# A gated-MLP kernel with attention ahead of it: the residual stream is remade from its normalized rows, which are turned by VectorE

## The chip, the cores and the metric

The kernel runs on one core of a Trainium2 chip. The metric is the device time of one execution in microseconds; several executions are timed and their median is told. A core has TensorE (PE, with a view of its own, PEld, for its weight loads), VectorE (DVE), ScalarE (ACT), GpSimd (POOL) and SyncE (SP), which here only issues DMA transfers. On-chip memory is SBUF (128 partitions) and PSUM, into which PE writes.

## The reference

Attention over a sliding window of 256 positions, its output projection, a residual, a layer norm, and a gated MLP whose gate mixes positions with a 2048 x 2048 matrix. The sizes are S = 2048 positions, D = 640, H = 32 heads, F = 1728 and Fh = F / 2 = 864; everything is float32.

```python
o = softmax(mask(q @ k.T * Dh ** -0.5)) @ v          # 32 heads, window 256
h = x + o @ wo                                       # residual stream
hn = _layernorm(h)
z = _gelu(hn @ w_in)
z1, z2 = z[..., :Fh], _layernorm(z[..., Fh:])
g = einsum("ts,bsf->btf", w_sp, z2) + b_sp
out = h + (z1 * g) @ w_out
```

h is used twice: normalized as the input of the MLP, and raw at the very end.

## The kernel before

Positions are worked in NT = 16 tiles of P = 128 rows; D is KD = 5 blocks of 128 columns. Each large product is made of three matmuls on parts: a number is split into a high part (a copy rounded to the matmul's format, by ACT) and a low part (the difference, mostly by VectorE), and high x high, high x low and low x high are summed. Some products are also cut into 2 x 2 blocks and done in seven products instead of eight, which needs sums and differences of blocks ahead of the split.

The stages, with their times in the profiled execution: attention up to 458.3 us, in a fixed order; then

- the projection (458.3 to 546.7), the loop over tiles i at lines 1325 to 1359. Tile i takes 30 matmuls (L96) into `wo_ps`, a PSUM accumulator of which there are three (`acc_tile`). VectorE adds x to it and makes the row sum in one instruction (L1345), which gives h in `xh` (five buffers, each reloaded with x, L142). ACT squares for the variance (L1348) and POOL takes the root (L1351). ACT writes the normalized rows hn(i) (L1356) into a buffer that is free by then: `rows[0]` or `rows[1]`, a quarter of `fx`, at the end `rows[2]`, `rows[3]`. h goes to DRAM as `h_d` on ACT's queue (L1349). The next tiles' o is loaded (L150), normalized (L166) and split (ACT L174, VectorE L175, into `xb`) in the same loop;
- three tiles later, `turn_h(i)` (L847) transposes hn(i) by five PE transposes (L856) into a PSUM tile of its own (`aux`, one buffer), ACT copies that to `ho` (L857, shown as L723), and SP stores it as `hn_d` (L858). The last three tiles are turned among the first z products;
- the z pairs 0 to 7 (`z_pair`, L872; 546.7 to 635.4) load two tiles of `hn_d` into quarters of `fx` (L889, L890), build sums, high and low parts in `aw`, multiply with `win1` (`zl`, made from w_in in the projection stage by `win1_prep`), apply the gelu and store z1;
- the z2 pairs 8 to 12 (`z2_pair`, L949; 635.4 to 692.1) do the same for the other half of w_in, load at L977, and make a layer norm of the result;
- the first gate (`first_gate`, to 825.8), the z2 pairs 13 to 15 (to 877), the second gate with the output projection (`second_gate`, `final`; to 1108.2), in which `load_h` (L1225) brings h back for the last sum. `turn_y` transposes the gated rows for the output projection and splits them (L137).

The order is written as steps. `at(n, f)` puts work f at step n; each step then issues its product. From the projection on, the framework orders the instructions of each engine by its own estimates of their durations, and every engine runs its list in that order. SP's list has all loads and nearly all stores; a DMA that stands behind one which still waits for its data waits as well. SP's DMAs go over eight completion lanes in turn. The 13th pair is special: its loads stand five steps ahead of its first product (`soon`), and its preparation one step ahead, since its buffers are not free earlier.

## Time and profile before

| | us |
|---|---|
| median of three executions | 1111.19 (1108.33 to 1111.58) |
| the profiled execution: its span from the first to the last instruction | 1108.2 |
| what lies around the span, by the median | 2.99 |
| projection stage | 88.4 |
| z pairs 0 to 7 | 88.7 |
| z2 pairs 8 to 12 | 56.7 |
| first gate | 133.7 |
| z2 pairs 13 to 15 | 51.2 |
| second gate and output | 231.2 |

The profile gives a span and no other time of its execution. The page shows, among other things, the busy share of each engine in 40 equal slices (27.7 us each; a digit is tenths, 9 is 90% or more); PEclk is the granted clock of TensorE:

```profile
PE   9999999999999999989999999999999999999998
DVE  6541212879999998677567478676637985566543
ACT  4333433249999999567776567433326531122210
POOL 3114444457777778512100055256422000000000
PEclk9999999999999999999999999999999999999999
DMA  7212565565666654678755421447593663444321
```

Slices 17 to 20 are the projection, 21 to 24 the z pairs. And the costliest transfers of hn_d and h_d, as the page's list of DMA issues has them (what, how many, KB each):

```profile
fx<-hn_d SPq DMA_DIRECT2D x32, 320.0 KB
```

### The profile page before, as it was taken

The page shows a single profiled execution, that of the slowest core. Times are in us where ns is not written, and L with a number is a line of the kernel's source. Part 1 is how long each engine was busy: PE and PEld are TensorE (multiplying, and loading weights), DVE is VectorE, ACT ScalarE, POOL GpSimd, SP SyncE. Part 2 cuts the span into 40 slices and gives each one's busy share as a digit, 9 for nine tenths or more (in the row PEclk, how much of TensorE's full clock was granted, in tenths as well). Part 3 has the DMA queues.
Part 4 walks back from the last instruction along what each step waited for, and adds up shares of the span by engine and source line. Part 5 has one row for each costly group of instructions (what it writes and reads, how often), then busy time and mean ns, then how long its engine had stood idle before and what let it go on. Part 6 is the DMA issues. An engine that isn't in the chain of part 4 may idle for free.

```text
span 1108.2 us, 27795 instructions
## 1 busy us (share of the span) xinstructions
PE 1084.3 (98%) x10667; PEld 974.4 (88%) x10667; DVE 720.7 (65%) x2043; ACT 571.0 (52%) x1215; POOL 369.6 (33%) x524
## 2 busy tenths in 40 slices
PE   9999999999999999989999999999999999999998
PEld 7998877668888877788899999999999999999998
DVE  6541212879999998677567478676637985566543
ACT  4333433249999999567776567433326531122210
POOL 3114444457777778512100055256422000000000
PEclk9999999999999999999999999999999999999999
DMA  7212565565666654678755421447593663444321
GB/s 261 74 35 96 166 221 179 196 210 181 214 204 214 215 177 120 193 254 281 242 188 193 151 80 39 165 154 233 190 339 113 204 215 114 129 132 150 100 91 65
DMA packets 88501, 187.80 MB, mean 169 GB/s; under 512 B 11648, under 2 KB 48144, under 8 KB 84448
## 3 DMA queue, kind: packets, MB, share of 16 engines
q1 hardware_dynamic: 83728, 172.08, 47.8%
q0 software_dynamic: 2336, 8.70, 2.2%
q10 hardware_dynamic: 2304, 5.24, 1.2%
q8 instruction: 84, 1.38, 0.5%
q14 instruction: 49, 0.40, 0.1%
HBM read 121.66 MB, written 65.52 MB: 169 GB/s over the span
## 4 chain that ended last, share of the span: by engine, by line
PE 78%; DMA 8%; DVE 3%; issue 3%; POOL 3%; ACT 3%; SPq 2%; ACTq 0%; POOLq 0%; DVEq 0%
PE g L1165 20%; PE zb L968 9%; PE out_ps L1218 8%; PE pv L435 6%; PE bank L341 5%; PE bank L407 5%; PE zx L916 3%; PE zv L916 2%; PE qk L525 2%; PE qk L526 2%; PE qk L527 2%; DMA qk_d<-sg 2%; PE zy L916 2%; SPq L320 1%; PE zw L916 1%
## 5 line engine op out<-in xcount | busy, mean ns | idle before, releaser
L410 ACT ACTIVATE pt<-bank 128x384 f32<-128x384 f32 (+2 forms) x512 | 200.8, 496 | 10.4 <-PE bank L407 5.7
L1165 PE MATMUL g<-zl,aw 128*128 128x432 f32 x768 | 169.7, 359 | 0.0
L353 DVE CUSTOM_DVE_ANT_0 junk<-bank,strip 128x288 bf16<-128x288 f32 x392 | 157.7, 454 | 4.3 <-PE bank L341 3.0
L723 ACT ACTIVATE aw<-fx 128x512 fp32r<-128x512 f32 (+2 forms) x147 | 84.9, 592 | 141.1 <-PE g L1165 101.9
L1165 PEld LDWEIGHTS g<-zl,aw 128*128 128x128 f32 x768 | 143.5, 188 | 6.1
L1165 PE MATMUL g<-ze,aw 128*128 128x432 f32 x576 | 131.9, 359 | 1.1 <-DVE row L717 1.1
L435 PE MATMUL pv<-pt,v_sb 128*32 128x192 f32 (+3 forms) x1984 | 127.3, 323 | 3.8 <-POOL pt L415 1.3
L717 DVE TENSOR_TENSOR aw<-fx,aw 128x512 fp32r<-128x512 f32 (+2 forms) x146 | 99.4, 690 | 28.6 <-ACT aw L723 23.5
L1165 PEld LDWEIGHTS g<-ze,aw 128*128 128x128 f32 x576 | 107.1, 188 | 6.2 <-DVE row L717 1.8
L407 PE MATMUL bank<-slot 123*32 123x288 bf16 (+5 forms) x1536 | 106.1, 282 | 1.0 <-ACT pt L410 0.4
L412 POOL TENSOR_SCALAR_AFFINE_SELECT pt<-pt 128x512 f32<-128x512 f32 x128 | 82.9, 648 | 43.6 <-ACT pt L410 42.4
L1218 PE MATMUL out_ps<-wout,y_sp 128*128 128x320 f32 (+1 forms) x630 | 96.4, 309 | 0.4 <-ACT y_sp L137 0.4
L968 PE MATMUL zb<-win,aw 128*128 128x432 f32 x480 | 95.0, 359 | 0.5 <-ACT aw L723 0.5
L1218 PEld LDWEIGHTS out_ps<-wout,y_sp 128*128 128x128 f32 (+1 forms) x630 | 94.2, 188 | 1.0 <-ACT y_sp L137 0.7
L968 PEld LDWEIGHTS zb<-win,aw 128*128 128x128 f32 x480 | 90.1, 188 | 5.0 <-ACT aw L723 0.9
L341 PE MATMUL bank<-slot 120*32 120x288 bf16 (+2 forms) x1264 | 89.8, 285 | 1.1 <-DVE mcol L353 1.0
L541 DVE TENSOR_TENSOR rest<-qk,sg 128x512 f32<-128x512 f32 x40 | 27.7, 692 | 86.1 <-ACT sg L539 86.1
L415 POOL TENSOR_SCALAR_AFFINE_SELECT pt<-pt 128x512 f32<-128x512 f32 x112 | 74.6, 666 | 0.0
L717 DVE TENSOR_TENSOR row<-g,row 128x432 f32<-128x432 f32 x80 | 48.2, 603 | 33.8 <-PE g L1165 30.3
L544 POOL TENSOR_TENSOR sg<-rest,sg 128x512 bf16<-128x512 f32 x40 | 46.6, 1166 | 69.2 <-ACT sg L543 60.2
L435 PEld LDWEIGHTS pv<-pt,v_sb 128*32 128x32 f32 x1984 | 59.5, 110 | 10.3 <-POOL pt L415 3.2
L407 PEld LDWEIGHTS <-slot 123*32 123x32 bf16 x1536 | 52.6, 96 | 16.2 <-issue 5.0
(216 smaller groups left out, 2195.1 us busy)
## 6 DMA issues: line engine op xcount, KB each, us to landing
fx<-wsp_in SPq DMA_DIRECT2D x30, 512.0 KB
slot<-qk_d SPq DMA_DIRECT2D x72, 200.0 KB
qk_d<-sg SPq DMA_DIRECT2D x32, 384.0 KB
slot<-qk_d SPq DMA_DIRECT2D x72, 160.0 KB
fx<-hn_d SPq DMA_DIRECT2D x32, 320.0 KB
o_d<-ot SPq DMA_DIRECT2D x64, 128.0 KB
z_d<-row SPq DMA_DIRECT2D x18, 432.0 KB
g_d<-row SPq DMA_DIRECT2D x16, 432.0 KB
```

What stands on the lines that cost most here:

```text
L341: nc.tensor.matmul(ps[32 * j:32 * j + 32, :n], part(st, half, 120, 0, hh, q0, 32), part(st, half, 120, 1, hh, lo + skip * j, n), start=Tru ...
L353: nc.vector.tensor_tensor_reduce(out=junk[:, :n], in0=ps[:, :n], in1=keep, scale=1.0, scalar=NEG, op0=OP.add, op1=OP.max, accum_out=m_cols ...
L407: nc.tensor.matmul(ps[32 * i:32 * i + 32, b:e], part(st, half, 123, 1, hh, k0, 32), part(st, half, 123, 0, hh, kb * P + b, e - b), start=T ...
L410: nc.scalar.activation(pt[:, hh, :n], ps[:, :n], AF.Exp, scale=SCALE)
L412: nc.gpsimd.affine_select(out=pt[:, :, :P], in_=pt[:, :, :P], pattern=[[0, 4], [1, P]], base=0, channel_multiplier=-1, compare_op=OP.is_ge ...
L435: nc.tensor.matmul(ps[32 * hh:32 * hh + 32, a - 512 * c:b - 512 * c], v_sb[:, kb, v0:v0 + 32], pt[:, hh, a - kb * P:b - kb * P], start=fir ...
L717: (eng or nc.vector).tensor_tensor(out=out, in0=a, in1=b, op=op)
L723: nc.scalar.activation(out, a, AF.Copy)
L916: nc.tensor.matmul(ps, a[x], b[:, y], start=start and m + x + y == 0, stop=stop and m == n - 1 and x == 1, skip_group_check=True)
L968: nc.tensor.matmul(b[0][:, :HF], a[t][:, x, kk], win2[0][:, y, kk, h * HF:(h + 1) * HF], start=kk + x + y == 0, stop=kk == KD - 1 and x == 1)
L1165: nc.tensor.matmul(ps, w[m][x][:, k], zc[k][m][:, y], start=start and k + x + y == 0, stop=stop and k == 3 and x == 1, skip_group_check=True)
L1218: nc.tensor.matmul(ps[j][:, :HD], src[:w, a, k, :], e1["wout"][:w, b, k, j * HD:(j + 1) * HD], start=(k == 0 and a + b == 0), stop=(k == K ...
```

## The change

h is no longer stored. Its mean and the reciprocal of its scale factor are kept per row in `hstat`, and at the end h is remade from the stored normalized rows as hn x std + mean, on ACT (`make_h`), in the buffer into which `load_h` now loads hn. The transposition by PE, its PSUM tile and `ho` go; the accumulators become four. The normalized rows are stored by one DMA right after they are made (`store_hn`) into an `hn_d` of four column bands of 160, so that each contiguous run is 640 bytes. A load (`load_hn`) is now four DMAs of 32 partitions each, one for each band; they place the four 32-row groups so that VectorE's transposition in blocks of 32 x 32 over the whole 128 x 640 buffer (`turn`) leaves the wanted columns on the partitions, in another order of columns. Readers take that order through a view of four dimensions (`turned`, `cols`), and the rows of w_in are reordered on the host to match. In `z_pair` the load moves from step 4q - 5 to 4q - 7 at the earliest and the turns get steps of their own; in `z2_pair` the turn precedes the high part. In `second_gate` `make_h` stands one to three steps behind its load.

```diff
     r_d = dram.tile([H, S], F32, name="r_d")
-    h_d = dram.tile([NT, P, D], F32, name="h_d")
     z1_d = dram.tile([NT, P, FH], F32, name="z1_d")
-    hn_d = dram.tile([NT, P, D], F32, name="hn_d")
+    hn_d = dram.tile([NT, 4, P, D // 4], F32, name="hn_d")
     g_d = dram.tile([NT, P, FH], F32, name="g_d")
...
     ones = const.tile([P, 2], F32, name="ones")
+    hstat = const.tile([P, 2, NT], F32, name="hstat")
...
     def acc_tile(name):
-        return pools["c"].tile([P, 2, 512], F32, tag="acc", bufs=3, name=name)
-
-    def aux_tile(name):
-        return pools["c"].tile([P, 2, 512], F32, tag="aux", bufs=1, name=name)
+        return pools["c"].tile([P, 2, 512], F32, tag="acc", bufs=4, name=name)
...
     mem["xh"].append(ep.tile([P, D], F32, name="xh4"))
-    mem["ho"] = [ep.tile([P, D], F32, name=f"ho{i}") for i in range(3)]
...
-    def turn_h(i):
-        ht = mem["ho"][i % 3]
-        if i < NT - 3:
-            ps = aux_tile(f"ht_ps{i}").rearrange("p a b -> p (a b)")
-            parts = [(0, KD, ps)]
-        else:
-            parts = [(0, 4, bank("b", f"ht_a{i}")), (4, KD, bank("b", f"ht_b{i}"))]
-        for k0, k1, ps in parts:
-            for k in range(k0, k1):
-                nc.tensor.transpose(ps[:, (k - k0) * P:(k - k0 + 1) * P], hn(i)[:, k * P:(k + 1) * P], ident)
-            copy(ht[:, k0 * P:k1 * P], ps[:, :(k1 - k0) * P])
-        nc.sync.dma_start(hn_d[i], ht)
+    def hn_rows(i):
+        return hn_d[i].rearrange("b p c -> p b c")
+
+    def store_hn(i):
+        nc.sync.dma_start(hn_rows(i), hn(i).rearrange("p (b c) -> p b c", b=4))
+
+    def load_hn(r, i):
+        for b in range(4):
+            nc.sync.dma_start(r[32 * b:32 * b + 32].rearrange("j (a c) -> j a c", a=4),
+                              hn_d[i, b].rearrange("(a j) c -> j a c", a=4))
+
+    def turn(r):
+        nc.vector.transpose(r, r)
+
+    def turned(r, k0=0, k1=KD):
+        return r.rearrange("p (a k j) -> p k a j", a=4, k=KD)[:, k0:k1]
+
+    def cols(t):
+        return t.rearrange("p (k a j) -> p k a j", a=4, j=32)
...
         s1 = view(fx, 4 * D, 256)
+        s1 = cols(s1)
         part = {n: (ah[:, o:o + l], al[:, o:o + l]) for n, o, l in
...
         def load():
-            nc.sync.dma_start(ri, hn_d[i])
-            nc.sync.dma_start(rj, hn_d[j])
-
-        a11, a12, a21, a22 = (r[:, o:o + 256] for r in (ri, rj) for o in (0, 256))
+            load_hn(ri, i)
+            load_hn(rj, j)
+
+        a11, a12, a21, a22 = (turned(r, k, k + 2) for r in (ri, rj) for k in (0, 2))
+
+        def hi(h, raw):
+            copy(cols(h), raw)
         def lo(h, l, raw):
-            minus(l, raw, h.bitcast(F32))
-
-        at(max(n0 - 13, 4 * q - 5), load)
-        at(max(n0 - 7, -4), lambda: copy(ah[:, :640], ri))
-        at(max(n0 - 6, -3), lambda: lo(ah[:, :640], al[:, :640], ri))
-        at(max(n0 - 5, -3), lambda: (plus(s1, a21, a22), copy(part[T1][0], s1), minus(a21, a11, a21)))
-        at(max(n0 - 4, -3), lambda: (minus(a11, s1, a11), minus(a12, a12, a11), copy(ah[:, 640:1152], ri[:, :512])))
+            minus(cols(l), raw, cols(h).bitcast(F32))
+
+        at(max(n0 - 13, 4 * q - 7), load)
+        at(max(n0 - 8, -5), lambda: turn(ri))
+        at(max(n0 - 7, -4), lambda: (turn(rj), hi(ah[:, :640], turned(ri))))
+        at(max(n0 - 6, -3), lambda: lo(ah[:, :640], al[:, :640], turned(ri)))
+        at(max(n0 - 5, -3), lambda: (plus(s1, a21, a22), hi(part[T1][0], s1), minus(a21, a11, a21)))
+        at(max(n0 - 4, -3), lambda: (minus(a11, s1, a11), minus(a12, a12, a11),
+                                     hi(ah[:, 640:1152], turned(ri, 0, 4))))
         at(n0 - 3, lambda: lo(*part[T1], s1))
-        at(n0 - 2, lambda: lo(ah[:, 640:1152], al[:, 640:1152], ri[:, :512]))
-        at(n0 - 1, lambda: copy(part[T3][0], a21))
-        at(n0, lambda: (lo(*part[T3], a21), copy(part["j"][0], rj[:, 512:])))
-        at(n0 + 1, lambda: (lo(*part["j"], rj[:, 512:]), copy(part[T4][0], a22)))
+        at(n0 - 2, lambda: lo(ah[:, 640:1152], al[:, 640:1152], turned(ri, 0, 4)))
+        at(n0 - 1, lambda: hi(part[T3][0], a21))
+        at(n0, lambda: (lo(*part[T3], a21), hi(part["j"][0], turned(rj, 4))))
+        at(n0 + 1, lambda: (lo(*part["j"], turned(rj, 4)), hi(part[T4][0], a22)))
         at(n0 + 2, lambda: lo(*part[T4], a22))
...
         def prep(t, first, eng):
-            r3 = r[t].rearrange("p (k t) -> p k t", k=KD)
+            h, l = (a[t][:, x].rearrange("p k (a j) -> p k a j", a=4) for x in range(2))
             if first:
-                copy(a[t][:, 0], r3)
+                turn(r[t])
+                copy(h, turned(r[t]))
             else:
-                minus(a[t][:, 1], r3, a[t][:, 0].bitcast(F32), eng)
+                minus(l, turned(r[t]), h.bitcast(F32), eng)
...
             soon = q == 13
-            at(m - (5 if soon else 12 if q == 8 else 6), lambda t=t, tile_t=tile_t: nc.sync.dma_start(r[t], hn_d[tile_t]))
+            at(m - (5 if soon else 12 if q == 8 else 6), lambda t=t, tile_t=tile_t: load_hn(r[t], tile_t))
             at(m - (1 if soon else 3), lambda t=t: prep(t, True, None))
...
     def load_h(n):
-        nc.sync.dma_start(e1["h"][n % 2], h_d[tile_of(n)])
+        nc.sync.dma_start(e1["h"][n % 2].rearrange("p (b c) -> p b c", b=4), hn_rows(tile_of(n)))
+
+    def make_h(n):
+        h, t = e1["h"][n % 2], tile_of(n)
+        nc.scalar.activation(h, h, AF.Identity, scale=hstat[:, 0, t:t + 1], bias=hstat[:, 1, t:t + 1])
...
         at(n0 + (11 if p == 0 else 7), lambda: load_h(j))
+        at(n0 + (11 if p == 0 else 8), lambda: make_h(i))
+        at(n0 + (13 if p == 0 else 8 if p == 7 else 10), lambda: make_h(j))
         gate_pair(p, 1, [add(11), add(22), add(12), add(12), add(22), add(11), add(21)], extra)
...
         ps = pre_ps[i] if i < 2 else proj_o(i, acc_tile(f"wo_ps{i}"))
-        if i > 2:
-            turn_h(i - 3)
         xt = hs.pop(i)
...
         nc.scalar.activation(hn(i), xt, AF.Square, bias=mv[:, 1:2], accum_out=mv[:, 2:3])
-        nc.scalar.dma_start(h_d[i], xt)
+        nc.scalar.activation(hstat[:, 1, i:i + 1], mv[:, 0:1], AF.Copy, scale=1.0 / D)
         nc.vector.tensor_scalar(out=mv[:, 2:3], in0=mv[:, 2:3], scalar1=1.0 / D, scalar2=EPS, op0=OP.mult, op1=OP.add)
...
         nc.vector.tensor_tensor(out=mv[:, 4:5], in0=mv[:, 1:2], in1=mv[:, 3:4], op=OP.mult)
+        nc.vector.reciprocal(out=hstat[:, 0, i:i + 1], in_=mv[:, 3:4])
         nc.scalar.activation(hn(i), xt, AF.Identity, scale=mv[:, 3:4], bias=mv[:, 4:5])
+        store_hn(i)
         next(w1, None)
...
         run(n)
-        if n < 3:
-            turn_h(NT - 3 + n)
         if n == 2:
...
     c = np.ascontiguousarray
+    w_in = np.asarray(B_w_in).reshape(4, KD, 32, 2 * FH).transpose(1, 0, 2, 3).reshape(D, 2 * FH)
     x = np.asarray(A_x)[0]
...
     w_out = np.pad(np.asarray(B_w_out), ((0, KF * P - FH), (0, 0)))
-    arrays = {"x_in": c(x), "wqk_in": c(wqk), "wv_in": c(wv), "wo_in": c(wo), "w_in_in": c(np.asarray(B_w_in)),
+    arrays = {"x_in": c(x), "wqk_in": c(wqk), "wv_in": c(wv), "wo_in": c(wo), "w_in_in": c(w_in),
               "wsp_in": c(wsp), "bsp_in": c(bsp), "w_out_in": c(w_out)}
...
     args = [nc.dram_tensor(n, a.shape, mybir.dt.from_np(a.dtype), kind="ExternalInput").ap()
```

Two places in the orders show what moves. The first is the end of the projection. On SP's list, where the last tiles come out, `xh` is the reload of x, `hn_d` the store of a tile's turned or, after the change, plain rows, `fx` a quarter buffer for a z pair; a row's first number is the line. Before:

```order
L142 DMA xh4_9594<-x_in 128x640
L858 DMA hn_d_70<-ho0_9595 128x640
L142 DMA xh0_8950<-x_in 128x640
L890 DMA fx_9623<-hn_d_70 128x640
L858 DMA hn_d_70<-ho1_9596 128x640
L858 DMA hn_d_70<-ho2_9597 128x640
```

After:

```order
L847 DMA hn_d_69<-fx_9620 128x4x160
L142 DMA xh2_8952<-x_in 128x640
L851 DMA fx_9620<-hn_d_69 32x4x160 x7
L847 DMA hn_d_69<-row0_9614 128x4x160
L142 DMA xh3_8953<-x_in 128x640
L851 DMA fx_9620<-hn_d_69 32x4x160
L847 DMA hn_d_69<-row1_9615 128x4x160
L142 DMA xh4_9594<-x_in 128x640
```

The stores come from the normalized rows themselves and stand between the pieces of the z pairs' loads, which now run through this part of the list in groups of four for one tile.

Still at the first place, VectorE's list at tile 13 (`mvc` are a row's statistics, `L1345` and, after the change, `L1359` the row sum of a tile). Before:

```order
L1345 ISA xh3_8953,mvc13_10343<-wo_ps13_10304,xh3_8953 128x640
L1345 ISA mvc13_10343 128x1
L717 TENSOR_TENSOR aw_9622<-fx_9623,aw_9622 128x512
L1347 TENSOR_SCALAR mvc13_10343<-mvc13_10343 128x1
L1350 TENSOR_SCALAR mvc13_10343<-mvc13_10343 128x1
L1355 TENSOR_TENSOR mvc13_10343<-mvc13_10343 128x1
L1345 ISA xh4_9594,mvc14_10394<-wo_ps14_10355,xh4_9594 128x640
```

After:

```order
L714 TENSOR_TENSOR aw_9619<-fx_9620,aw_9619 128x512
L855 STREAM_TRANSPOSE fx_9620<-fx_9620 128x640
L1364 TENSOR_SCALAR mvc12_10229<-mvc12_10229 128x1
L1359 ISA xh3_8953,mvc13_10294<-wo_ps13_10263,xh3_8953 128x640
L1359 ISA mvc13_10294 128x1
L1369 TENSOR_TENSOR mvc12_10229<-mvc12_10229 128x1
L1370 RECIPROCAL hstat_82<-mvc12_10229 128x1
L714 TENSOR_TENSOR aw_9619<-fx_9620,aw_9619 128x640
L1361 TENSOR_SCALAR mvc13_10294<-mvc13_10294 128x1
L855 STREAM_TRANSPOSE fx_9620<-fx_9620 128x640
```

A turn now stands ahead of the row sum of tile 13, and the next one ahead of that of tile 14; in all six turns stand ahead of the last row sum, at tiles 10, 11, 13, 14 and, two, 15.

The second place is pair 13, behind the first gate. It shows first on SP's list (`g_d` is the gate's store, `ze` a reload of parts that are made early). Before:

```order
L1184 DMA g_d_71<-row2_9619 128x864
L1070 DMA ze4_10532<-zp_d_75 128x864
L977 DMA fx_9623<-hn_d_70 128x640
L1185 DMA g_d_71<-row3_9620 128x864
L977 DMA fx_9623<-hn_d_70 128x640 x2
L1070 DMA ze3_10531<-zp_d_75 128x864
```

After:

```order
L1194 DMA g_d_70<-row2_9616 128x864
L1080 DMA ze4_10443<-zp_d_74 128x864
L851 DMA fx_9620<-hn_d_69 32x4x160
L1195 DMA g_d_70<-row3_9617 128x864
L851 DMA fx_9620<-hn_d_69 32x4x160 x4
L1080 DMA ze3_10442<-zp_d_74 128x864
L851 DMA fx_9620<-hn_d_69 32x4x160 x7
```

Twelve pieces stand where three loads stood, and the last seven of them stand behind the second `ze` reload, three of them pieces of the pair's second row block. It shows also on VectorE's list, where `g0_6` and `g0_7` are the gate's products in PSUM that are added into `row` and `aw` takes low parts. After:

```order
L714 TENSOR_TENSOR fx_9620<-fx_9620 128x512
L714 TENSOR_TENSOR aw_9619<-fx_9620,aw_9619 128x512 x2
L714 TENSOR_TENSOR row1_9615<-g0_7_0_0_12662,row1_9615 128x432
L714 TENSOR_TENSOR row0_9614<-g0_7_1_1_12680,row0_9614 128x432
L855 STREAM_TRANSPOSE fx_9620<-fx_9620 128x640 x2
L714 TENSOR_TENSOR aw_9619<-fx_9620,aw_9619 128x640
```

Both turns come ahead of the low part of the first block (the `aw` row behind them).

## The prediction

> **What bounds the kernel now.** I read the page's first part, then a table of busy time by stage, then what TensorE (PE) waits for in the stage that the change empties. The page first (engine, busy us, share of the span, instructions):
>
> ```profile
> span 1108.2 us, 27795 instructions
> PE 1084.3 (98%) x10667; PEld 974.4 (88%) x10667; DVE 720.7 (65%) x2043; ACT 571.0 (52%) x1215; POOL 369.6 (33%) x524
> ```
>
> PE is the bound. A change gains by taking instructions off PE or by ending PE's waits, and loses by giving PE a new wait. Where it idles is seen in the table of stages (the columns are named in its first line). The rows are: the projection, the z pairs 0 to 7, the z2 pairs 8 to 12, the first gate, the z2 pairs 13 to 15, the second gate with the output.
>
> ```profile
> core 0: us, PE busy (x) PEld busy (x) DVE busy (x) ACT busy (x) POOL busy (x), PEclk, DMA share, GB/s
> 458.30:546.70 88.40, 80.45 (x564) 77.34 (x561) 58.29 (x147) 53.58 (x95) 13.86 (x16) 1.00 0.80 262
> 546.70:635.40 88.70, 88.70 (x463) 84.90 (x461) 55.30 (x116) 57.08 (x107) 2.25 (x2) 1.00 0.54 180
> 635.40:692.10 56.70, 56.70 (x290) 54.33 (x289) 45.04 (x83) 38.80 (x69) 31.62 (x27) 1.00 0.20 64
> 692.10:825.80 133.70, 132.06 (x672) 125.55 (x671) 82.16 (x122) 49.31 (x88) 58.25 (x72) 1.00 0.61 208
> 825.80:877.00 51.20, 51.19 (x260) 48.86 (x261) 38.15 (x81) 29.54 (x49) 8.97 (x9) 1.00 0.50 176
> 877.00:1108.20 231.20, 227.33 (x1377) 221.57 (x1376) 129.28 (x245) 49.85 (x99) 0.00 (x0) 1.00 0.41 128
> ```
>
> Only the projection has idle time that this change touches: 88.40 - 80.45 = 7.95 us. The granted clock is 1.00 in every stage. The view of PE's waits in that window (what waited, for what, us in total, times, longest) puts nearly all of it down to the transposes that the change deletes:
>
> ```profile
> PE ht_ps L856 <- ACT ho L723: 4.9, 3, 2.6
> PE ht_ps L856 <- ACT row L1356: 2.8, 2, 1.9
> ```
>
> **Projection stage: what goes.** The timeline of PE (start, us, group, wait before it) gives the price of one tile's five transposes on PE:
>
> ```profile
> 490.48 0.77 PE L856 MATMUL ht_ps<-ident,row 128*128 128x128 f32 x5 [1.92 <-ACT row L1356]
> 491.00 0.82 PE L96 MATMUL wo_ps<-xb 128*128 128x320 f32 x4
> ...
> 546.23 0.77 PE L856 MATMUL ht_ps<-ident,row 128*128 128x128 f32 x5 [2.58 <-ACT ho L723]
> 546.75 1.43 PE L916 MATMUL zv<-zl,aw 128*128 128x432 f32 x6
> 548.02 0.60 PE L856 MATMUL ht_a<-ident,row 128*128 128x128 f32 x4
> ```
>
> Matmuls overlap, so the price is from start to start: 491.00 - 490.48 = 0.52 us (0.52 again at 546.23). Thirteen tiles lie in this stage: 13 x 0.52 = 6.8 us of PE work that goes. The two waits are 4.9 + 2.8 = 7.7 us. Together 14.5 us, which would leave a stage of 73.9 us. The last three tiles' transposes lie among the z products (the row at 548.02): 3 x 0.52 = **1.6 us**, on a PE that never idles there, so these go in full.
>
> **What is late next.** VectorE (DVE) gains work: a turn for each row block, and 16 reciprocals. The trace has no turn. The nearest rows of a 128x640 pass are these (group, count, busy us, mean ns, idle before):
>
> ```profile
> L86 DVE TENSOR_SCALAR xn<-xt,mva 128x640 f32<-128x640 f32 x16 | 9.8, 611 | 9.4 <-POOL mva L83 9.4
> L717 DVE TENSOR_TENSOR aw<-fx,aw 128x640 fp32r<-128x640 f32 x16 | 13.9, 871 | 14.6 <-ACT aw L723 14.6
> L1345 DVE CUSTOM_DVE_ANT_0 xh<-wo_ps,xh 128x640 f32<-128x640 f32 x16 | 13.1, 818 | 2.1 <-PE wo_ps L96 2.1
> L717 POOL TENSOR_TENSOR aw<-fx,aw 128x640 fp32r<-128x640 f32 x8 | 13.5, 1693 | 88.5 <-ACT aw L723 88.4
> L1355 DVE TENSOR_TENSOR mvc<-mvc 128x1 f32<-128x1 f32 x15 | 2.4, 157 | 4.4 <-POOL mvc L1351 4.3
> L1356 ACT ACTIVATE row<-xh,mvc 128x640 f32<-128x640 f32 x10 | 9.2, 915 | 2.3 <-DVE mvc L1355 2.0 <-DVE mvc L1350 0.2
> ```
>
> A turn is bounded by 0.61 us (VectorE's quickest pass of this shape) and 1.69 us (the slowest elementwise pass of it on any engine). I take **0.82**, by the two VectorE rows of 818 and 871 ns, since I see no reason for it to be as quick as the pass with one operand. A reciprocal of 128x1 I put at 0.16 (row L1355), between 0 and twice that. Six turns stand in VectorE's queue before z starts: 58.29 + 6 x 0.82 + 16 x 0.16 = 65.8 us of the 73.9 that PE would need. So VectorE still fits by its sum, at 89%, but it runs in order. The Trainium skill, page "VectorE: DVE Perf Modes", section "The three transpose paths", gives 311 ns for a VectorE transpose of 128x128 in bf16 against 390 ns on TensorE, and its rules for kernel authors say to use TensorE for a full 128x128. By it a turn would be five of these, an estimate of 1.56 us, with which the sum below would come out 3 us above the time of before; no trace here shows which holds.
>
> ScalarE (ACT) gets freer:
>
> ```profile
> L723 ACT ACTIVATE ho<-ht_ps x13: 676/682/708, 483.5 to 547.0; 128x640 f32<-128x640 f32 x13
> ```
>
> Thirteen copies of 0.68 us go (8.9 us, least, median and longest ns in the row) and sixteen copies of one column come.
>
> The order matters more than the sum. The turns of pair 1's rows (fx[2], fx[3], in which tiles 10 and 11 were normalized) stand in VectorE's queue ahead of the row sums of tiles 13 and 14. Each must wait until hn(10) or hn(11) has been stored and the buffer loaded again. The chain of waits shows how long a 320 KB transfer takes here (start, us, what):
>
> ```profile
> 483.08 7.66 DMA h_d<-xh
> 538.88 5.14 DMA fx<-hn_d
> ```
>
> A store and a load are 7.7 + 5.1 = 12.8 us, while two tiles of a 73.9 us stage are 2 x 73.9 / 16 = 9.2 us. The turn is then 3.6 us late, and tile 13's row sum behind it too. With half as much again for the second row I lose 5.5 of the 14.5 us and take a net gain of **9.0**. Its bounds are a loss of 1 (every wait comes back under another name) and a gain of 14.5 (spare accumulators, four in place of three, swallow the lateness).
>
> **DMA engines.** The projection is also the stage in which they are busiest (0.80). The views of queues in three windows (packets, MB, share of 16 engines; first 440 to 560 us, then 445 to 449, then 454.9 to 457) give their prices:
>
> ```profile
> q10 hardware_dynamic: 2304, 5.24, 11.4%
> ```
>
> ```profile
> q1 hardware_dynamic: 839, 0.77, 62.8%
> ```
>
> ```profile
> q1 hardware_dynamic: 183, 0.09, 15.0%
> ```
>
> q10 carries the h_d stores alone: 11.4% of 120 us x 16 = 219 engine-us, / 16 = 13.7 us of all engines that go, 0.86 a store. A packet took 48 ns at 0.77 MB / 839 = 918 bytes (62.8% of 4 x 16 us, over 839) and 28 ns at 492 bytes, so 640 bytes I put at 34 ns: a transfer of 512 runs is 512 x 0.034 / 16 = 1.09 us where it was 0.86 (bounds 0.90 and 1.54). Sixteen stores and eight loads add 24 x 0.23 = 5.5 us, so the engines gain 8 us net. They do not become the bound, and I book nothing. The Trainium skill, page "DMA: Bandwidth & Descriptors", section "Anatomy of one DMA", fits 2.0 us plus bytes over 436 GB/s to a transfer on another path, an estimate of 8.8 us for four pieces of 80 KB in series against 2.8 for one; with that the pair 1 turn would be another 6 us later. Against that speak two rows of this trace (SP's timeline and the chain of waits):
>
> ```profile
> 475.49 3.18 SPq L150 DMA_DIRECT2D m<-o_d  x5
> ```
>
> ```profile
> 496.46 5.24 DMA m<-o_d
> ```
>
> Five such loads are issued in 3.18 us, less than the 5.24 that one takes to land: transfers of one queue overlap, and so will four pieces.
>
> **z and z2 stages.** VectorE gets at most 14 turns in the first (55.30 + 11.5 = 66.8 of 88.70) and 10 in the second (45.04 + 8.2 = 53.2 of 56.70). PE never waited in either, though a load of hn_d already kept VectorE up to 2.93 us:
>
> ```profile
> 591.84 0.88 DVE L717 TENSOR_TENSOR fx<-fx 128x256 f32<-128x256 f32 x2 [2.93 <-DMA fx<-hn_d]
> ```
>
> The cover is VectorE's slack, 33 and 12 us; it is gone at (88.7 - 55.3) / 14 = 2.4 us a turn in the one and (56.7 - 45.04) / 10 = 1.17 in the other. I book **+0.5 each** for a turn that comes late once (0 to 3).
>
> **Pair 13.** Its loads and its preparation are put close together. SP's timeline, then ACT's and PE's:
>
> ```profile
> 817.55 0.45 SPq L1185 DMA_DIRECT2D g_d<-row  x1
> 818.09 1.26 SPq L977 DMA_DIRECT2D fx<-hn_d  x2
> 819.46 4.43 SPq L1070 DMA_DIRECT2D ze<-zp_d  x3
> ...
> 825.02 0.74 ACT L723 ACTIVATE aw<-fx 128x640 fp32r<-128x640 f32 x1 [1.43 <-DMA fx<-hn_d]
> ...
> 825.81 24.49 PE L968 MATMUL zb<-win,aw 128*128 128x432 f32 x123 [0.50 <-ACT aw L723]
> ```
>
> Here PE already waits for the load (0.50 us). After the change the first row block needs four issues (three more at about 0.32 to 0.63 us, about 1.0) and a turn (0.82): 1.8 us later. VectorE turns the second block, too, before it makes the first one's low part, and that block's last three pieces stand behind a ze load (4.43 / 3 = 1.5 us): 1.8 + 1.5 = **+3.3** (0 to 8).
>
> **Second gate.** ACT gets 16 x 0.915 = 14.6 us beside 49.85 in 231: hidden, and the h loads stay where they were. The last is close:
>
> ```profile
> 1090.21 0.32 SPq L1225 DMA_DIRECT2D row<-h_d  x1
> ...
> 1092.68 0.60 ACT L137 ACTIVATE aw<-yt_ps 128x512 fp32r<-128x512 f32 x1 [1.11 <-PE yt_ps L1205]
> ...
> 1098.41 6.34 PE L1218 MATMUL out_l<-wout,aw 128*128 128x320 f32 x42
> ```
>
> make_h(15) stands on ACT ahead of that split: 1090.21 + 5.14 + 0.92 + 0.60 = 1096.9, before PE wants it at 1098.41. I book 0 (0 to 2).
>
> **Sum.** 1108.2 - 9.0 - 1.6 + 0.5 + 0.5 + 3.3 = 1101.9 us of span. The median of the runs, 1111.19, lies 2.99 above the profiled span, so I predict 1101.9 + 2.99 = **1105 us**.
>
> **Rivals.**
> - *VectorE keeps up*: the fourth accumulator hides the late turns, the stage gives 14.5 and pair 13 costs at most its 3.3. The span is 1108.2 - 14.5 - 1.6 + 1.0 + 3.3 = 1096.4, the run 1099; without pair 13's cost 1096. For it: 11% of spare VectorE. Against it: in-order turns behind a 12.8 us round trip.
> - *The waits only change their name*, so the change does not take out the time that it says: PE loses its transposes but waits for the low part at L175, and 4 of 14.5 us are gained: 1105 + 5 = 1110.
> - *VectorE's queue is held by the round trip* (slower): the rows of pairs 1 and 2 come late in each of the last four tiles, each by the 3.6 us above, so 14.4 us eat up the stage's gain, and pair 13 costs 6. Then 1111.2 - 1.6 + 1.0 + 6 = 1116.6. It decides for slower once the stage's loss passes 14.5 + 1.6 - 1.0 - 3.3 = 11.8 us, about 3 us at each of four tiles. For it: the round trip is longer than two tiles. Against it: SP can issue loads early, and stores no longer share engines with h_d.
> - *A turn costs 1.69*: 0.87 more for each of 8 on the path (6 in the projection, 2 at pair 13), 7.0, and z2 then needs 45.04 + 16.9 = 61.9 for 56.7, 4.7 beyond what is booked: 1105 + 11.7 = 1117. It decides from about 1.4 us a turn. The estimate from the Trainium skill's transpose figures falls between this and the forecast.
>
> **How the numbers follow.** About 0.3% (3.3 us) is what a measurement of this kernel can tell from no change. Forecast 0.43, VectorE keeps up 0.16 (both faster); waits with another name 0.20 (same); held queue 0.14 and dear turn 0.07 (slower). Faster 0.59, same 0.20, slower 0.21. The range runs from 1096 (stage bound, pair 13 at nothing) to 1115, which leaves out most of the two slower cases and little below.
>
> **What would show it.** Right: no PE wait at a transposition; the projection some 9 us shorter; PE's busy time about 8 us smaller; a STREAM_TRANSPOSE group of 32 at about 820 ns; PE waiting 2 to 5 us at pair 13's first product. Wrong: a turn well over 1.2 us; PE waiting for the low part of xb (L175) through the whole old gap; new waits of PE among the z products; out_l starting late for the last split. The prediction falls if a load of hn_d arrives much later than the one before, so that it holds VectorE for longer than 3.6 us.

## The result: slower, and the profile after

| | median us | range | runs |
|---|---|---|---|
| before, timed beside it | 1108.33 | 1107.42 to 1111.58 | 5 |
| after | 1116.52 | 1114.91 to 1118.83 | 5 |

The ratio is 1.0066, 95% interval 1.0045 to 1.0086: the change costs about 0.7%, where 1105 us was forecast (1096 to 1115). The profiled execution took 1116.94 us with a span of 1115.2. The first part of the page after, with the chain of waits by engine, and below it the chain before:

```profile
span 1115.2 us, 27849 instructions
PE 1079.3 (97%) x10587; PEld 968.6 (87%) x10587; DVE 743.9 (67%) x2091; ACT 575.7 (52%) x1228; POOL 367.7 (33%) x524
PE 63%; DMA 12%; DVE 10%; issue 5%; ACT 4%; POOL 4%; SPq 3%; DVEq 0%; POOLq 0%; ACTq 0%
```

```profile
PE 78%; DMA 8%; DVE 3%; issue 3%; POOL 3%; ACT 3%; SPq 2%; ACTq 0%; POOLq 0%; DVEq 0%
```

PE is busy for 5.0 us less (1084.3 before), and the span is 7.0 us longer: PE waits 12 us more. The chain, 78% PE and 11% VectorE and DMA before, is 63% PE and 22% VectorE and DMA now. The table of stages tells where. It is cut at PE's first product of each stage, the last time behind the gate's last product: projection, z and z2 pairs up to 12, first gate, and all from pair 13 on. Before:

```profile
458.30:546.75 88.45, 80.50 (x565) 77.39 (x562) 58.34 (x147) 53.58 (x95) 13.86 (x16) 1.00 0.80 262
546.75:691.90 145.15, 145.15 (x750) 138.98 (x749) 100.09 (x198) 95.67 (x175) 33.87 (x29) 1.00 0.41 135
691.90:825.30 133.40, 132.26 (x673) 125.74 (x672) 82.35 (x121) 49.05 (x88) 58.25 (x72) 1.00 0.61 207
825.30:1108.20 282.90, 278.52 (x1637) 270.43 (x1636) 167.44 (x326) 79.85 (x149) 8.97 (x9) 1.00 0.42 137
```

After:

```profile
459.10:541.70 82.60, 73.94 (x501) 72.24 (x497) 59.51 (x158) 46.93 (x94) 10.36 (x15) 0.98 0.76 226
541.70:692.40 150.70, 146.99 (x732) 138.07 (x733) 112.00 (x221) 91.03 (x168) 35.05 (x30) 0.99 0.41 125
692.40:829.50 137.10, 132.72 (x673) 125.63 (x672) 88.27 (x130) 51.79 (x94) 58.88 (x72) 1.00 0.59 201
829.50:1115.20 285.70, 279.25 (x1636) 270.28 (x1636) 171.41 (x331) 93.35 (x165) 8.92 (x9) 1.00 0.44 136
```

The projection is 5.9 us shorter, the z stages 5.5 longer, the first gate 3.7, and the rest 2.8; attention ended 0.8 later. Together that is the 7.0 us, but for rounding. The z stages should have lost 1.6 us of transposes, so 7.1 us in them are new: PE waits 3.7 us there (it never did before), and is busy for 3.4 us more than without the transposes, of which a slower clock explains about half (below). VectorE (the third figure behind the length) works 12 us more there, and 6 us more in the first gate, in whose stretch the change puts one turn on it: it seems to carry work over. The waits of VectorE for these loads, from the start of z to the first gate, show why (total, times, longest), first before and then after, and below them the group of the turns:

```profile
DVE fx L717 <- DMA fx<-hn_d: 4.9, 4, 2.9
```

```profile
DVE fx L855 <- DMA fx<-hn_d: 24.5, 18, 3.1
```

```profile
L855 DVE STREAM_TRANSPOSE fx<-fx 128x640 f32<-128x640 f32 x32 | 27.0, 844 | 34.6 <-DMA fx<-hn_d 34.4
```

A turn takes 844 ns, as was forecast (820), but VectorE stands still in front of 24 of the 32 until the last piece of a load lands. The waits of PE from attention's end on name the places:

```profile
PE wo_ps L96 <- DVE xb L175: 3.3, 3, 1.8
PE zv L925 <- DVE mvc L1359: 3.0, 1, 3.0
PE wo_ps L96 <- DVE mvc L1364: 2.4, 1, 2.4
PE g L1175 <- ACT row L720: 2.0, 1, 2.0
PE zb L978 <- DVE aw L714: 1.7, 1, 1.7
```

The third line belongs to no turn: the first turn runs at 522.87, and this wait ends at 475.60. The row sum of tile 1 stands behind a pass of L166 there, which normalizes attention's output o and waits 6.76 us for a load; PE, whose next tile takes the same accumulator, waits for the row sum (the profile names L1364, the small instruction right behind it). VectorE's two rows and PE's:

```profile
473.24 1.56 DVE L166 TENSOR_TENSOR m<-m 128x640 f32<-128x640 f32 x2 [6.76 <-DMA m<-r_d]
474.71 0.82 DVE L1359 CUSTOM_DVE_ANT_0 xh<-wo_ps,xh 128x640 f32<-128x640 f32 x1
```

```profile
475.60 0.57 PE L96 MATMUL wo_ps<-xb 128*128 128x320 f32 x2 [2.36 <-DVE mvc L1364]
```

Before, the row sum stood ahead of that pass, and PE did not wait:

```profile
468.07 0.82 DVE L1345 CUSTOM_DVE_ANT_0 xh<-wo_ps,xh 128x640 f32<-128x640 f32 x1 [2.09 <-PE wo_ps L96]
473.51 1.56 DVE L166 TENSOR_TENSOR m<-m 128x640 f32<-128x640 f32 x2 [4.61 <-DMA m<-r_d]
```

The costliest place is the start of z. VectorE's timeline there (rows between are left out):

```profile
535.89 0.85 DVE L855 STREAM_TRANSPOSE fx<-fx 128x640 f32<-128x640 f32 x1 [2.00 <-DMA fx<-hn_d]
...
536.69 0.81 DVE L1359 CUSTOM_DVE_ANT_0 xh<-wo_ps,xh 128x640 f32<-128x640 f32 x1
...
539.13 0.84 DVE L855 STREAM_TRANSPOSE fx<-fx 128x640 f32<-128x640 f32 x1 [0.68 <-DMA fx<-hn_d]
...
540.82 0.80 DVE L1359 CUSTOM_DVE_ANT_0 xh<-wo_ps,xh 128x640 f32<-128x640 f32 x1
```

and PE's, with the table's row for the 3.7 us behind its start:

```profile
541.69 2.53 PE L925 MATMUL zv<-zl,aw 128*128 128x432 f32 x6 [3.02 <-DVE mvc L1359]
```

```profile
541.50:545.20 3.70, 3.51 (x10) 3.24 (x11) 2.86 (x10) 1.98 (x6) 0.35 (x1) 0.54 0.49 146
```

Tile 14's row sum (540.82) stands behind a turn (539.13), which waits for its load; in the order as built this is the first turn of pair 2, and the one at 535.89, ahead of tile 13's row sum, is the first of pair 1. The first z product writes the PSUM bank in which tile 14 was accumulated, and so waits for that row sum. PE idles for 3 us, and then runs 3.7 us at a granted clock of 0.54: six products take 2.53 us there, 1.43 before. Cut finely, the slow stretch is 3.4 us at 0.50, in which PE does the work of half that time; so about 1.7 us, an estimate, are lost that no wait shows. The wait at 475.60 has such a stretch behind it, too, from 476.8 to 480.2. The Trainium skill, page "TensorE: Matmul & The Clock Gate", part 1, says that an idle window of about 3.4 us puts the clock to half until a busy one has passed, and that the windows run freely. This trace agrees on the half and on the length of the slow stretch; but its two waits, 3.02 and 2.36 us, are shorter than such a window (see the last section).

What feeds the turns is a round trip. The chain of waits at that place (pieces under 0.1 us, and others at the dots, are left out):

```profile
529.10 3.37 DMA hn_d<-fx
532.48 0.32 SPq L851
532.85 0.42 SPq L851
533.33 0.42 SPq L851
...
534.32 0.38 SPq L851
534.80 2.74 DMA hn_d<-fx
...
539.32 2.84 DMA fx<-hn_d
542.38 0.85 DVE fx L855
```

The normalized rows of a tile are stored (3.37 us for tile 10's), and only then can the loads into the same buffer be issued, at some 0.43 us a piece, with the next store in the same queue; the load for the turn at 539.13 stands behind them. The chain ends in the turn at 542.38, ahead of tile 15's row sum, for which PE waits another 1.2 us.

### The profile page after: what moved, and what is told of

The parts are those of the page before. It is cut to its first block, busy times and chain, and to the rows that moved or that the text cites. A ratio compares the mean times of both kernels' runs of the same rounds, so it can differ in the third digit from the quotient of the medians.

```text
span 1115.2 us, 27849 instructions
## 1 busy us (share of the span) xinstructions
PE 1079.3 (97%) x10587; PEld 968.6 (87%) x10587; DVE 743.9 (67%) x2091; ACT 575.7 (52%) x1228; POOL 367.7 (33%) x524
## 4 chain that ended last, share of the span: by engine, by line
PE 63%; DMA 12%; DVE 10%; issue 5%; ACT 4%; POOL 4%; SPq 3%; DVEq 0%; POOLq 0%; ACTq 0%
PE g L1175 20%; PE out_ps L1228 8%; PE pv L435 6%; PE bank L341 5%; PE bank L407 5%; DMA fx<-hn_d 4%; PE qk L525 2%; PE qk L526 2%; PE qk L527 2%; DMA qk_d<-sg 2%; DVE row L714 2%; DVE aw L714 2%; SPq L851 2%; POOL sg L544 1%; ACT pt L410 1%
```

## The experiments

Ratios are to the kernel before, timed on the same chip beside each. Its own median there lies between 1108.3 and 1111.6 us, so kernels of different chips are compared by their ratios: 0.001 is 1.1 us, and a ratio is known to about 0.002. Stage times are those of one profiled execution each. Four things could have made it slower: late loads (A), the work of the turns (B), stores that hold loads in SP's queue (C), and the accumulators' banks (D). Remaking h (E) and the order (F) came up on the way.

**Single loads.** hn_d keeps the order that a turn needs; the store is in four parts (as is the load of it at the end), the load for a turn is one.

```diff
-    hn_d = dram.tile([NT, 4, P, D // 4], F32, name="hn_d")
+    hn_d = dram.tile([NT, P, D], F32, name="hn_d")
...
+    def hn_rows(i, a):
+        return hn_d[i].rearrange("(b j) (a c) -> a j b c", b=4, a=4)[a]
+
+    def bands(r, a):
+        return r[32 * a:32 * a + 32].rearrange("j (b c) -> j b c", b=4)
...
-        nc.sync.dma_start(hn_rows(i), hn(i).rearrange("p (b c) -> p b c", b=4))
+        for a in range(4):
+            nc.sync.dma_start(hn_rows(i, a), bands(hn(i), a))
...
-        for b in range(4):
-            nc.sync.dma_start(r[32 * b:32 * b + 32].rearrange("j (a c) -> j a c", a=4),
-                              hn_d[i, b].rearrange("(a j) c -> j a c", a=4))
+        nc.sync.dma_start(r, hn_d[i])
```

> The four pieces are moved from the load to the store: hn_d keeps rows in the order that a turn needs, so that each load is one DMA of 128 x 640 with 2560-byte runs, and each store (and each load of h at the end) is four DMAs of 32 partitions. Theory A (the turns hold VectorE's queue because four-part loads land late): VectorE's idle time ahead of the turns, 34.4 us in the changed kernel, falls below 20 us, the gap ahead of the first z product shrinks, and the time falls from 1116.5 to about 1111. Theory B (the work of the turns itself, 32 x 0.845 = 27 us, overloads VectorE): the waits change but the time stays within 1.5 us of 1116.5. Theory C (stores that wait for ScalarE hold the loads behind them in SP's queue): stores now take four issues, so 1117 to 1119.

1112.74 us, ratio 1.0021 (1.0004 to 1.0038). The idle time ahead of the turns falls from 34.6 to 20.3 us, the z stages take 146.6 us (150.7 with pieces), and the first gate 134.2 (137.1). But the projection takes 86.8 (82.6 with pieces): PE waits 3.1 us for xb and 4.6 ahead of z, each time with half the clock behind it. Its stores now need four issues each, which may be why. By the ratios some 5 us come back. A holds behind the projection.

**Stores on ScalarE's queue.** `nc.sync` becomes `nc.scalar` in `store_hn`.

> Only the stores of the normalized rows move, from SP's queue to ScalarE's, where the store of h was before. Theory C (stores hold the loads in SP's queue): SP issues the loads earlier, the idle time ahead of the turns of the projection's end (4.3 us) falls below 2, z starts 2 us earlier, and the time is 1112 to 1114. Theories A and B: under 1.5 us of change, 1115 to 1118.

1120.84 us, 1.0087 (1.0058 to 1.0117), no faster than the changed kernel: as far as this edit tests it, C falls.

**Turns with little work.** `nc.vector.transpose(r[:, :32], r[:, :32])`; the other columns stay as they were loaded.

> Each turn covers 32 columns instead of 640 (the rest of a row block is left as it was loaded), so that its place and its waits stay and its work goes from 0.845 us to some 0.1. Theory A (waits): at most 2 us faster, 1114.5 or more, with the idle time ahead of the turns still above 30 us. Theory B (work): about 24 us of VectorE's time go, and with them most of the loss behind the projection (7 us in the z pairs, 3.5 in the first gate): 1108 or less.

1113.25 us, 1.0027 (1.0005 to 1.0050). The idle time ahead of the turns is still 32.9 us. The first gate takes 134.6 us, but the z stages 149.6. By the ratios some 4 us come back, between what A and B gave; the two intervals, this one and the change's, just touch. So the work is a part of the loss, and not all of it.

**Both.**

> one_load with turns of 32 columns only (the rest of a row block is left as loaded): late loads and the work of the turns are both taken away. If waits and work cost separately, the gains add: 1116.5 - 3.8 - 3.3 = 1109.4. If both are the same lateness of VectorE, counted twice: 1112 to 1113.

1110.32 us, 0.9996 (0.9974 to 1.0018): 0.0070 below the change, where adding the two gives 0.0084. As far as intervals of 0.002 tell, late loads and work are mostly separate costs.

**Turns one step later** in the z pairs' program (`turn(ri)` at n0 - 7, `turn(rj)` at n0 - 6).

> In the z pairs the two turns stand one step later (the first one just ahead of the copy that reads it, the second one behind the first low part), so that a load has a step more to land. Theory A: the idle time ahead of the turns falls by 5 to 10 us and the time by 2 to 4, to about 1113. Theory B: within 1.5 us of 1116.5. Theory C: no change in the projection, under 2 us in all.

1119.39 us, 1.0077 (1.0052 to 1.0103), with 35.7 us idle ahead of the turns: a miss. In its trace the turns stand ahead of the same row sums as in the change (one ahead of tile 13's, one ahead of tile 14's, two ahead of tile 15's): the step in the program did not set a turn's place, the framework's order did.

**Another bank for the first product.** The accumulators become four tags of one buffer each, and the tiles take them in the order 0,1,2,3,1,2,3,0,1,2,0,3,2,1.

> Only the accumulators' places change: the last tiles take the four in another order, so that the first z product writes a PSUM bank that tile 12 held, and no longer one of tile 14's, whose row sum stands behind a turn. Theory D (the gap ahead of z, and the clock of about half behind it, come from that bank): the gap ahead of the first z product falls from 3.3 us to under 1.5, the granted clock behind it stays near 1, and the run is 2 to 4 us faster than 1116.5. Rival (VectorE's backlog sets the pace wherever PE meets it): the gap moves to the next products and the time stays within 1.5 us.

1117.69 us, 1.0061 (1.0039 to 1.0082). In its profile z starts without a gap and at clock 1.00, but PE then waits 1.3 and 2.0 us for row sums, and 1.2 for ScalarE, ahead of the following products. D names where PE met the lateness, and its rival holds: moving the meeting place gains nothing. Single loads with this order:

> one_load and banks together. Theory A with D: the loss of one_load (1112.7) was mostly at the gap ahead of z (4.9 us and the slow clock behind it), so 1107 to 1110. Rival: as one_load, 1111 to 1114.

1112.66 us, 1.0027 (1.0003 to 1.0051): the rival again.

**h kept.** `h_d`, its store on ScalarE's queue and its load come back; `make_h`, the copy and the reciprocal go. Then the same with single loads and the other banks:

> Half of the change is undone: h is stored on ScalarE's queue and loaded at the end as before, and not remade; the statistics' copies and reciprocals go. The turns and the four-part loads stay. Theory A: within 2 us of 1116.5, with the idle time ahead of the turns still above 30 us. Rival E (remaking h costs, by ScalarE's 16 x 0.9 us in the second gate and the reciprocals on VectorE): 1113 or less.

> one_banks with h stored and loaded as before: single loads of turned-order rows, the other order of accumulators, no remaking. Theory A: within 1.5 us of one_banks, since remaking h is hidden. Rival E: 3 us or more below one_banks.

1111.44 us, 0.9997 (0.9974 to 1.0020), and 1112.48 us, 1.0017 (0.9989 to 1.0045). The first missed theory A's forecast: by the ratios 0.7% comes back with h. The second met it: on the same chip it ran 0.2 us below its twin without h. In the first, the scheduler put the row sums of tiles 13 and 14 ahead of all four turns of the pairs 1 and 2, while each stands behind one of them in the changed kernel. So the result mixes h with an order. First the small instructions alone:

```diff
-        nc.scalar.activation(hstat[:, 1, i:i + 1], mv[:, 0:1], AF.Copy, scale=1.0 / D)
-        nc.vector.reciprocal(out=hstat[:, 0, i:i + 1], in_=mv[:, 3:4])
+        nc.gpsimd.tensor_tensor(out=hstat[:, 1, i:i + 1], in0=mv[:, 0:1], in1=root[:, 1:2], op=OP.mult)
+        nc.gpsimd.tensor_tensor(out=hstat[:, 0, i:i + 1], in0=mv[:, 2:3], in1=root[:, 0:1], op=OP.pow)
```

> h is remade as in the changed kernel, but its two statistics are made by GpSimd (a product and a power of one column for each tile) and no longer by ScalarE (copy) and VectorE (reciprocal). Rival E1 (the loss by h lies in these small instructions, which stand in the two in-order queues of the projection): the projection falls from 82.6 us to 78 to 80 as it did with h kept, and the time to 1112 to 1114. Rival E2 (it lies elsewhere: the final make_h, or the order into which the scheduler put the rest): 1115 to 1118.

1117.16 us, 1.0058 (1.0034 to 1.0082): nothing.

**The order itself.** A factor of 1 that is computed from tile 15's row sum ties the four turns of the pairs 1 and 2 behind it.

```diff
+        nc.vector.tensor_scalar(out=g, in0=col, scalar1=1.0, scalar2=1.0, op0=OP.max, op1=OP.min)
...
+            nc.vector.tensor_scalar(out=r[:, :1], in0=r[:, :1], scalar1=gates[g], scalar2=None, op0=OP.mult)
         nc.vector.transpose(r, r)
...
+        if i == NT - 1:
+            gate(mv[:, 0:1])
```

> The four turns of the pairs 1 and 2 are made to depend on tile 15's row sum (a one-column factor of exactly 1 that is computed from it), so that the scheduler can no longer put them, and their waits for loads, ahead of the row sums of tiles 13 to 15. Nothing else is changed. Theory F (these turns hold the row sums, and with them the PSUM accumulators into which the first z products write): the gap ahead of z falls from 3.3 us to under 1.5, the granted clock behind it stays at 1, and the time falls by 3 to 5 us to 1112 to 1113. Rival (VectorE has too much work there in any order): the wait moves to the next products, 1115 to 1118.

1109.61 us, 0.9982 (0.9961 to 1.0004). This is 0.0084, some 9 us, below the change, more than theory F's 3 to 5, for five more VectorE instructions of one column. From the kernel before it can't be told apart. Its stages, PE's first z products and VectorE's turns:

```profile
457.80:536.20 78.40, 73.87 (x500) 72.16 (x496) 57.44 (x156) 46.05 (x93) 10.33 (x15) 0.98 0.77 231
536.20:684.00 147.80, 144.97 (x733) 137.13 (x734) 115.58 (x229) 92.50 (x170) 35.00 (x30) 1.00 0.43 131
684.00:820.60 136.60, 132.66 (x673) 125.48 (x671) 87.25 (x129) 51.33 (x92) 60.31 (x72) 1.00 0.59 201
```

```profile
536.21 1.46 PE L934 MATMUL zv<-zl,aw 128*128 128x432 f32 x6 [0.52 <-DVE mvc L1368]
```

```profile
540.06 1.56 DVE L864 STREAM_TRANSPOSE fx<-fx 128x640 f32<-128x640 f32 x2
```

Projection 78.4 (82.6 in the change), z stages 147.8 (150.7); the first gate's 3.2 us of loss stay. The gap ahead of z is 0.5 us, six products take 1.46 us again, and the turns come at 540.06, with their loads landed. The wait for tile 1's row sum (2.3 us, with the slow clock behind it) is there as in the change. The same with pair 13's second turn tied behind the first low part:

> gated, and at pair 13 the turn of the second row block is made to depend on the first block's low part, so that it no longer stands ahead of it. Theory F: PE's second wait at pair 13 (1.7 us) goes, 1.5 to 2 us below gated. Rival: the wait goes over to the second block's products, same as gated.

1110.78 us, 0.9988 (0.9965 to 1.0010). PE's second wait at pair 13 is gone in the profile, but the run is not faster than gated: 2 us can't be told apart there.

**Order and loads, order and h.**

> one_load (single loads, stores in four parts) with the turns of the pairs 1 and 2 behind tile 15's row sum. Theories A and F together: the gap ahead of z (4.9 us in one_load, with the slow clock behind it) goes, 3 to 5 us below one_load's 1112.7: 1108 to 1110, no slower than the kernel before. Rival: 1111 to 1114.

> gated_all with h stored and loaded as before the change and not remade. The order of row sums and turns is then the same with and without the remaking. Theory F (h_kept gained because the scheduler happened to put tile 14's row sum ahead of the turns there): within 1.5 us of gated_all. Rival E (remaking h itself costs): 3 to 5 us below gated_all.

1107.58 us, 0.9969 (0.9947 to 0.9990), and 1107.15 us, 0.9956 (0.9935 to 0.9977). Both are faster than the kernel before, by 0.3 and 0.4%. Against gated_all, on the same chip, keeping h is 3.6 us faster, so F does not seem to explain all of h_kept; but the two intervals overlap a little. Whether the statistics are that part, and whether everything adds up:

> gated_all with the two statistics of h made by GpSimd instead of ScalarE and VectorE. gated_all ran at 1110.8 and, with h kept, at 1107.2. If the small statistics instructions on the two in-order queues are that difference: 1107 to 1108.5. If they are not: 1110 to 1112.

> All that gave something: single loads with stores in four parts, turns behind the row sums of tile 15 and behind the low part at pair 13, h stored and loaded as before. If the causes add (single loads 2 to 4 us, keeping h 3.5): 1103 to 1105 beside 1111 before. If they share one lateness: 1106 to 1108, as the better of one_gated and hkept_gated_all.

1111.15 us, 1.0010 (0.9988 to 1.0031): the statistics' engines are not it. 1111.76 us, 0.9995 (0.9974 to 1.0016): both forecasts missed, the causes don't add; its projection takes 83.3 us, with four-part stores and the stores of h.

Why keeping h gains 3.6 us with the turns held back stays open, but the traces say where to look. The projection takes 76.4 us in hkept_gated_all and 80.1 in gated_all, where PE waits 2.9 us for tile 1's row sum and then has half the clock for 3.4 us. In the traces of all 13 kernels that remake h this row sum stands behind the pass that waits for a load, as shown above; in all seven that store h it stands ahead. No run has this order alone, so it is a likely part of the gain and not a shown one.

**Two more tries.** Stores in four parts from GpSimd's queue, with h kept; and the kernel before with its transposes one tile later (in it, tile 11's rows are overwritten by pair 1's load ahead of their transposition).

> h kept, single loads, four-part stores issued by GpSimd instead of SP, accumulators as in the changed kernel. Theory A (late loads, and VectorE's queue behind them): the z pairs lose under 2 us, SP's loads of o are no longer behind stores, 1107 to 1110. Rival: the four-part stores still come late, 1111 to 1114.

> The kernel before with each tile's transposition one tile later (four tiles behind instead of three, the last four among the z products). If PE's 7.7 us of waits ahead of the transpositions are for work that is merely one tile late, 1104 to 1108 beside 1111 before; if they are ScalarE's backlog, within 1.5 us of before.

1121.65 us, 1.0099 (1.0069 to 1.0129): the projection takes 93.3 us. 1110.31 us, 0.9997 (0.9978 to 1.0015): PE's waits for the transposes before were not for work that is one tile late.

## Why the prediction was wrong, point by point

- **The mechanism of the loss was on record, as the rival "VectorE's queue is held by the round trip"** (1116.6, measured 1116.5), with a chance of 0.14. Its split was wrong: it put the whole loss into the projection, which gained 5.9 us, and left the z stages and the first gate nearly alone. That its total fits is luck.
- **Projection, -9.0:** mis-sized, measured -5.9. PE's busy time there fell by 6.6 us, with 6.8 booked; the term that failed is the waits. The forecast took a lateness of 3.6 us and half as much again, 5.5, for turns ahead of the last row sums. PE waits 8.7 us: 3.0 for tile 14's row sum, which was late as forecast; 3.3 for xb (L175), as in the rival "the waits only change their name"; and 2.4 at 475.6, behind a load that has nothing to do with turns. gated, in which the turns stand behind the row sums, gained 10.0 us. Without lateness the forecast was 14.5; PE's remaining 4.5 us of waits in that stage are the difference. (The forecast named pair 1's turns ahead of the row sums of both tiles 13 and 14; ahead of tile 14's it is pair 2's.)
- **z and z2, +0.5 each:** this is the step that failed. The cover was worked out from busy time (55.30 + 11.5 us of 88.70, gone at 2.4 us a turn), as if VectorE could always work. It was idle for 24.5 us ahead of turns (4.9 us on such loads before), with all that is queued behind. Measured +5.5 in place of -0.6 for the two stages with their transposes: 3.7 us of it are waits of PE, and some 1.7 the slow clock behind the gap ahead of z, for which the forecast had no price. In their profiles one_load gives back 4.1 us, gated 2.9.
- **First gate, put at nothing without a reason:** +3.7 us. What VectorE did not do in z2 it seems to do here (nine more instructions, one of them a turn). With single loads (134.2 us) or turns of little work (134.6) most of it is gone.
- **Pair 13, +3.3:** about right. Everything from there on is 2.8 us longer, with PE's two waits of 0.8 and 1.7 us where they were expected.
- **Second gate and make_h, 0:** no wait of PE for make_h appears; the output's one wait, on ScalarE's split, is 0.4 us as before.
- **The sum:** 3.1 us more in the projection than forecast, 6.1 in the z stages, 3.7 in the first gate, 0.5 less from pair 13 on, and 0.8 at attention's end, which the change does not touch, make 13.2 of the 13.3 us between the span forecast (1101.9) and measured (1115.2). The 2.99 us around the span were too many: this execution shows 1.7 (1116.94 - 1115.2), so the span of before was that of an execution below the median.
- **The price of a turn** (0.82) was right: 0.844. The Trainium skill's figures, page "VectorE: DVE Perf Modes", section "The three transpose paths", gave an estimate of 1.56 us; the measurement decides.
- **The sum of the DMA engines** moved as forecast: 0.80 before, 0.76 in the projection after.
- **Four pieces of a load** overlap, as forecast: they are issued at 0.43 us each, and the last landed 2.84 us behind its issue.
- **That PE's transposes and their waits go** was right; the new waits on L175 (3.3 us), on row sums behind turns (3.0) and at 475.6 (2.4) took the places of 7.7 us. PE's busy time fell by 5.0 us and not by 8: two slow stretches at half clock hold 3.4 us of it.

## What to carry to other kernels

An instruction that waits for a load is as long, for everything behind it in an in-order queue, as the wait and the work together: add up the waits, not the busy time, before calling an engine's slack a cover. When work moves from the engine that is the bound to one that is 65% busy, ask which small instruction of that engine the bound waits for, and look up in the built order what stands ahead of it; here a tie of one column put it right and was worth 0.8%. A step number in the program is no guarantee of a place in the built order. And compare all places where the order changed, not only those that the change is about: tile 1's row sum moved, too.

## What the runs showed of the hardware

A gap of PE can cost more than its length, and no fixed length decides it. From one product's start to the next, the gap ahead of z was 3.33 us in the change, 4.94 in one_load and 2.85 in short_turn; each time the granted clock was about half for the next 3.5 us (0.50 in one_load, 0.55 in short_turn). In the kernel before, 2.89 us at the same place left it at 1.00.

By these traces, what decides is where the gap falls. In each of the 20, by their records of the granted clock, it changes only at whole multiples of 3.41 us from its other changes: in the change it is half from 476.82 to 480.24 and again from 541.68 to 545.09, and the two starts lie 64.86 us, 19 x 3.41, apart. The rows of these windows and of the ones just ahead of them show PE's busy time as the second figure and the clock as the third from the end:

```profile
473.41:476.82 3.41, 1.22 (x8) 1.23 (x9) 3.39 (x8) 2.33 (x5) 0.84 (x1) 1.00 0.51 155
476.82:480.24 3.42, 3.42 (x15) 3.42 (x14) 3.42 (x8) 2.12 (x5) 0.00 (x0) 0.50 0.65 183
538.26:541.68 3.42, 0.41 (x3) 0.14 (x1) 2.03 (x8) 1.92 (x4) 0.55 (x1) 1.00 0.82 224
541.68:545.09 3.41, 3.40 (x9) 3.14 (x10) 2.62 (x8) 1.80 (x6) 0.24 (x1) 0.50 0.49 147
```

Before, whose clock is half from 244.7 to 248.1, the same step puts the gap ahead of z across two windows, and the clock stays:

```profile
541.65:545.06 3.41, 2.00 (x15) 1.73 (x14) 0.41 (x2) 1.02 (x2) 0.30 (x1) 1.00 0.84 283
545.06:548.47 3.41, 2.24 (x16) 2.14 (x17) 2.65 (x7) 2.56 (x6) 0.00 (x0) 1.00 0.52 201
```

Cut like this from 300 us on, the 20 traces have 27 windows at full clock with PE busy for less than 1.5 us, and a slow one follows each; of the 4348 with more than 1.8 us none is followed by one; of the 23 between, six are. So in this kernel about half a window of work keeps the clock up. A gap close to 3 us costs some 1.7 us more or nothing, by how it falls on the windows. That fits the free-running windows of the page on TensorE in the Trainium skill that is named above. Its table speaks of an idle window; here 1.22 us of work in a window did not keep the clock up, and the measurement decides.
